# Merging the two root exponentials of a unit, replacing the roots' check by minima, and splitting one copy, in an attention and MLP kernel

## The chip, the cores and the metric

One core of one Trainium2 chip. The metric is the device time of one execution in microseconds (us), median of several runs. A profiled execution of the same program gives the trace; its span is some 1.8 us shorter than the time (605.9 against 607.63 us before). Engines are called PE (TensorE), PEld (its weight loads), ACT (ScalarE), DVE (VectorE), POOL (GpSimd) and SP.

## The reference

Attention with normalised queries and keys (8 batches, 12 heads, 448 positions, 64 columns), then a residual MLP with a layer norm:

```python
def rmsnorm(x, g):
    return x / np.sqrt(np.mean(x * x, axis=-1, keepdims=True) + 1e-06) * g
q_n, k_n = rmsnorm(q, g_q), rmsnorm(k, g_k)
scores = (1.0 / np.sqrt(64)) * np.matmul(q_n, k_n.transpose(0, 1, 3, 2))
attn = softmax(scores)                        # cut: written out with its maximum
x = np.matmul(attn, v) ...                    # to (8, 448, 768)
xn = (x - mu) / np.sqrt(var + 1e-06) * g_ln
out = x + np.maximum(xn @ w_ch1, 0.0) @ w_ch2 # 768 -> 3072 -> 768
```

## The kernel before

Heads are handled in 48 pairs, and the pairs in 25 units (units 0 and 1 hold one pair, the others two). A unit's preparation squares and sums queries and keys, takes the inverse roots, splits the scaled keys in a high and a low half (`khl`) and scales the queries (`qn`). Units 0 to 5 are prepared by a hand-written order at the start, while there is little MLP work to fill PE. The keys' root isn't multiplied into the keys: it is the per-row scale of the score exponential.

```python
def root(n=slice(0, 2)):                      # of unit u; n: queries, keys or both
    nc.scalar.activation(c["rt"][:, n], c["ssq"][:, n], AFT.Ln, bias=D * 1e-6)
    for i in range(2)[n] if isinstance(n, slice) else (n,):
        nc.scalar.activation(c["r", i], c["rt"][:, i], AFT.Exp, scale=-0.5)
# c["r", 0]: a rotating tile "rq" (2 buffers); c["r", 1]: 14 columns of self.rr,
# which keeps the keys' roots of all units (336 columns)

def trans_q(self, p):                         # seven transposes on PE, then one copy
    ...
    if p in ACT_Q:                            # ACT_Q = (0, 1)
        nc.scalar.copy(out=qT, in_=ps.rearrange("p e s -> p (e s)"))

def scores(self, p, i):
    ...                                       # i = 0, 1, 2 use head 0, then 3, 4, 5 head 1, 6 both
    nc.scalar.activation(out=c["E"][:, i], in_=ps[:, 0:S], func=AFT.Exp,
                         scale=self.rr[:, g:g + 1], bias=EXP_BIAS)

def flag(self):                               # near the end: was every root in range?
    ...
    nc.vector.tensor_scalar(out=good[:, 0:nk], in0=self.rr, scalar1=sh.gmax,
                            scalar2=None, op0=ALU.is_ge)
```

The end of the hand-written order, where `M` computes `gmax` on DVE, `m5` duplicates queries, `V6.6` ends pair 6's values, and `K7` transposes and copies pair 7's keys:

```
... N2 R Q7 X2 c5 e5 j5 g5 k5 l5 z5 U1 U2 V6.5 M m5 V6.6 L7 K7
```

Of the kernel before, what the change touches and what calls it, by code (L numbers as in the profile page):

```python
# [8 lines left out]
FP32 = mybir.dt.float32  # L9
FP16 = mybir.dt.float16  # L10
INT32 = mybir.dt.int32
ALU = mybir.AluOpType
AFT = mybir.ActivationFunctionType
AX = mybir.AxisListType
# [7 lines left out]
NPAIR = H // 2  # L22
# [53 lines left out]
class _Fast:  # L76


    def __init__(self, ctx, tc, sh, q, k, v, gs, g_ln, w1, w2, out):
        self.gs, self.g_ln = gs, g_ln  # L80
        self.tc, self.nc, self.sh = tc, tc.nc, sh
        self.q, self.k, self.v, self.w1, self.w2, self.out = q, k, v, w1, w2, out
        nc = tc.nc
        pool = lambda name, bufs, **kw: ctx.enter_context(tc.tile_pool(name=name, bufs=bufs, **kw))
        self.p_in = pool("p_in", 2)
        self.p_n = pool("p_n", 2)
        self.p_e = pool("p_e", 2)
        self.p_x = pool("p_x", 2)
        self.p_xl = pool("p_xl", 2)
        self.p_m = pool("p_m", 1)  # L90
        self.fix = pool("fix", 1)
        self.ps_tr = pool("ps_tr", 1, space=PSUM)
        self.ps_s = pool("ps_s", 2, space=PSUM)
        self.ps_o = pool("ps_o", 1, space=PSUM)
        self.ps_m = pool("ps_m", 3, space=PSUM)
        fix = self.fix
        self.kU = [fix.tile([128, 1920], FP16, name=f"kU{i}", tag=f"kU{i}") for i in range(2)]
        self.qU = [fix.tile([128, 2, 2, S], FP16, name=f"qU{i}", tag=f"qU{i}") for i in range(2)]
        self.v16 = fix.tile([128, 6, 2, 3, D + 1], FP16, name="v16", tag="v16")
        self.vl = fix.tile([128, 6, 2, D + 1], FP16, name="vl", tag="vl")  # L100
        nc.vector.memset(self.v16[:, :, :, :, D], 1.0)
        nc.vector.memset(self.vl, 0.0)
        nc.vector.memset(self.vl[0:64, :, 0, D], 1.0)
        nc.vector.memset(self.vl[64:128, :, 1, D], 1.0)
        self.rec = fix.tile([128, B * NPAIR, 4, 2], FP32, name="rec_all", tag="rec_all")
        nc.vector.memset(self.rec, 0.01)
        self.rr = fix.tile([128, 7 * B * NPAIR], FP32, name="rr_all", tag="rr_all")
        self.rs = fix.tile([128, B, 4], FP32, name="rs_all", tag="rs_all")
        nc.vector.memset(self.rs, RS_LO)
        self.hT = fix.tile([128, NFF, 512], FP16, name="hT", tag="hT")  # L110
        self.tr = self.ps_tr.tile([128, 1024], FP16, name="tr", tag="tr")
        nc.vector.memset(self.tr[:, 64:128].bitcast(FP32), 0.0)
        self.zero_left(DMA_UNIT)
        self.xs, self.xls, self.st = {}, {}, {}
        self.units, self.loads, self.prs = {}, {}, {}
        self.late, self.preps = [], {}
# [71 lines left out]
    def pieces(self, u):  # L188
# [9 lines left out]
        def begin():  # L198
            c["t"] = self.loads.pop(u)
            c["ssq"] = self.p_n.tile([128, 2, 14], FP32, tag="ssq", name="ssq")[:, :, 0:g]  # L200
            c["rt"] = self.p_n.tile([128, 2, 14], FP32, tag="rt", name="rt")[:, :, 0:g]
            o = 7 * UNIT_PAIR[u]
            c["r", 0] = self.p_n.tile([128, 14], FP32, tag="rq", name="rq")[:, 0:g]
            c["r", 1] = self.rr[:, o:o + g]
            c["qn"] = self.p_n.tile([128, 14, 2, D], FP16, tag="qn", name="qn")[:, 0:g]
            c["khl"] = self.p_n.tile([128, 14, 2, D], FP16, tag="khl", name="khl")[:, 0:g]
            self.units[u] = (c["qn"], c["khl"], m)

        def square(n):

# [8 lines left out]

        def root(n=slice(0, 2)):  # L220
            nc.scalar.activation(c["rt"][:, n], c["ssq"][:, n], AFT.Ln, bias=D * 1e-6)
            for i in range(2)[n] if isinstance(n, slice) else (n,):
                nc.scalar.activation(c["r", i], c["rt"][:, i], AFT.Exp, scale=-0.5)  # L223

        def kg():
            if u == 0:
# [81 lines left out]
    def trans_k(self, p):  # L308
        nc, sh = self.nc, self.sh
        u, w = PAIR_UNIT[p]  # L310
        qn, khl, m = self.units[u]
        kT, ps = self.kU[PE_SET][:, 960 * (p % 2):960 * (p % 2) + 960], self.tr
        nc.tensor.matmul(ps[:, 0:256].rearrange("p (e o) -> p e o", e=2)[:, :, 0:D],
                         khl[:, self.group(p, 6)], sh.id16, is_transpose=True, start=True, stop=False)
        for i in range(6):
            nc.tensor.matmul(ps[:, 192 + 128 * i:320 + 128 * i], khl[:, self.group(p, i)], sh.id16,  # L316
                             is_transpose=True, start=False, stop=(i == 5))
        nc.vector.tensor_copy(out=kT, in_=ps[:, 0:960])

    def trans_q(self, p):  # L320
        nc, sh = self.nc, self.sh
        u, w = PAIR_UNIT[p]
        qn, khl, m = self.units[u]
        tr = self.ps_m.tile([128, 1024], FP16, tag="mlp", name="psQ") if p < NPAIR else self.tr
        ps = tr[:, 128:128 + 2 * S].rearrange("p (e s) -> p e s", e=2)
        qT = self.qU[PE_SET][:, p % 2].rearrange("p e s -> p (e s)")
        nc.tensor.matmul(ps[:, :, 384:S], qn[:, self.group(p, 6)], sh.id16, is_transpose=True,
                         start=True, stop=False)
        for i in range(6):
            nc.tensor.matmul(ps[:, i // 3, ts(i % 3, 128)], qn[:, self.group(p, i)], sh.id16,  # L330
                             is_transpose=True, start=False, stop=(i == 5))
        if p in ACT_Q:
            nc.scalar.copy(out=qT, in_=ps.rearrange("p e s -> p (e s)"))
        else:
            nc.vector.tensor_copy(out=qT, in_=ps.rearrange("p e s -> p (e s)"))
        kT = self.kU[PE_SET][:, 960 * (p % 2):960 * (p % 2) + 960]
        self.prs[p] = dict(q=qT, main=kT[:, 192:960], left=kT[:, 0:192])

    def scores(self, p, i):

        nc = self.nc
        c = self.prs[p]
        q, left = c["q"], c["left"]
        if i == 0:
            c["E"] = self.p_e.tile([128, 7, S], FP16, tag="E", name="E")
        if p > UNIT_PAIR[DMA_UNIT] and (7 * p + i) % 3 == 2:
            ps = self.ps_tr.tile([128, 512], FP32, tag="tr", name="psS3")
        else:
            ps = self.ps_s.tile([128, 512], FP32, tag="psS", name="psS")
        if i < 6:  # L350
            h = i // 3
            nc.tensor.matmul(ps[:, 0:S], c["main"][:, ts(i, 128)], q[:, ts(h, S)],  # L352
                             start=True, stop=True)
        else:
            nc.tensor.matmul(ps[:, 0:S], left[:, 0:128], q[:, 0:S], start=True, stop=False)  # L355
            nc.tensor.matmul(ps[:, 0:S], left[:, 64:192], q[:, S:2 * S], start=False, stop=True)  # L356
        g = 7 * UNIT_PAIR[PAIR_UNIT[p][0]] + self.group(p, i)
        nc.scalar.activation(out=c["E"][:, i], in_=ps[:, 0:S], func=AFT.Exp,  # L358
                             scale=self.rr[:, g:g + 1], bias=EXP_BIAS)

    def values(self, p, i):
        nc = self.nc
# [50 lines left out]
    def first_attention(self):  # L413
# [7 lines left out]
        for x in ORDER:  # L421
# [12 lines left out]
            elif key in "SV":  # L434
                (self.scores if key == "S" else self.values)(*map(int, n.split(".")))
            elif key in "KQT":
                dict(K=self.trans_k, Q=self.trans_q, T=self.stats)[key](int(n))
            elif key in "ANXR":
                ln = ln or self.ln_ops(0)
                ln[x]()  # L440
            elif key == "M":
                gmax = self.sh.gmax
                nc.vector.tensor_reduce(out=gmax, in_=self.sh.gprod, axis=AX.X, op=ALU.max,
                                        apply_absolute_value=True)
                nc.vector.tensor_scalar(out=gmax, in0=gmax, scalar1=1.0 / K_MAX, scalar2=None,
                                        op0=ALU.mult)
            elif key == "U":
                self.up_first(int(n))
            elif key == "H":
                ps = self.ps_m.tile([128, 512], FP32, tag="mlp", name="psW")  # L450
                for _ in range(int(n)):
                    nc.tensor.matmul(ps[:, 0:384], self.sh.id16,
                                     self.v16.rearrange("p s h j d -> p (s h j d)")[:, 0:384],
                                     start=True, stop=True)
            else:
                self.prep_ops(int(x[-1]))[x[:-1]]()
# [480 lines left out]
```

## Time and profile before

| | before |
|---|---|
| time, median of the first three runs | 607.91 us (607.86 to 608.15) |
| span of the profiled run | 605.9 us |
| PE busy / PE's first key transpose / PE without waits from | 578.3 us / 8.49 us / 66.04 us |

The page gives busy time and share of the span by engine; the slices divide the span in 40, and a 9 is 90% or more. A line of the timeline is: start, duration, engine, source line, operation, output, input, and in brackets the idle time just before it and what ended that. Two rows of PE, from the timeline of PE between 60 and 67 us:

```profile
60.93 0.55 PE L352 MATMUL psS<-qU,kU 128*128 128x448 f16 x2 [0.46 <-DVE kU L318]
66.04 0.35 PE L352 MATMUL psS<-qU,kU 128*128 128x448 f16 x1 [0.17 <-ACT E L358]
```

The first are the first scores of pair 7, which waited for DVE's copy of the keys. The second are the sixth scores of pair 7, which waited for an exponential of ACT. After this row PE never waits again: I call it PE's steady point.

### The profile page before, as it was taken

The numbers are of one execution on the slowest core, as the hardware profiler recorded it, in microseconds if no ns is written. First come the engines' busy times: TensorE is split into PE (matmuls) and PEld (weight loads), VectorE is DVE, ScalarE is ACT, GpSimd is POOL, SyncE is SP. The second block draws the span as 40 slices with busy tenths as digits, with TensorE's granted clock in tenths as the row PEclk, the third lists the DMA queues.
The fourth block names the chain that finished last, engine by engine and source line by source line (L and its number), as shares of the span: only waits on it lengthen the run. The fifth ranks groups of instructions, "written<-read, shape, count | busy, mean of one in ns | idle before, by whom it ended". The sixth has DMA issues, their size and how long they took to land.

```text
span 605.9 us, 11525 instructions
## 1 busy us (share of the span) xinstructions
PE 578.3 (95%) x4500; PEld 344.6 (57%) x4500; DVE 286.5 (47%) x618; ACT 360.7 (60%) x697; POOL 189.5 (31%) x245
## 2 busy tenths in 40 slices
PE   2877999999999999999999999999999999999995
PEld 1555666655566666655566666655566666654564
DVE  5799567734346256715256255734256322540011
ACT  6996986278752697358753598548754477124200
POOL 3853432233551355332542345423512000000000
PEclk9999999999999999999999999999999999999998
DMA  9999999479864586844944585847722330130011
GB/s 208 266 213 217 215 224 178 123 195 87 143 157 117 98 129 146 177 135 83 150 121 113 123 125 128 197 116 121 133 65 70 92 62 2 34 98 0 1 53 57
DMA packets 130861, 75.29 MB, mean 124 GB/s; under 512 B 96656, under 2 KB 121040, under 8 KB 130800
## 3 DMA queue, kind: packets, MB, share of 16 engines
q1 hardware_dynamic: 114048, 45.12, 38.3%
q0 software_dynamic: 16080, 28.94, 21.6%
q8 instruction: 37, 0.61, 0.4%
q10 hardware_dynamic: 672, 0.43, 0.2%
q14 instruction: 24, 0.20, 0.1%
HBM read 52.36 MB, written 11.01 MB: 105 GB/s over the span
## 4 chain that ended last, share of the span: by engine, by line
PE 88%; DVE 1%; ACT 1%; issue 0%
PE psC L637 36%; PE psH L621 34%; PE psS L352 8%; PE oA L381 5%; PE oB L383 2%; PE psS L356 1%; PE psS L355 1%; PE tr L330 0%; PE tr L316 0%; ACT E L358 0%; DVE x L398 0%; DVE qn L67 0%; DVE khl L240 0%; ACT khl L215 0%; ACT hT L623 0%
## 5 line engine op out<-in xcount | busy, mean ns | idle before, releaser
L621 PE MATMUL psH<-xnT,w 128*128 128x512 f16 (+1 forms) x1134 | 241.9, 353 | 0.0
L358 ACT ACTIVATE E<-psS,rr_all 128x448 f16<-128x448 f32 x336 | 207.0, 634 | 48.3 <-PE psS L352 43.0
L637 PE MATMUL psC<-w,hT 128*128 128x384 f16 (+1 forms) x1368 | 234.7, 323 | 0.0
L623 ACT ACTIVATE hT<-psH 128x512 f16<-128x512 f32 (+1 forms) x189 | 104.0, 550 | 123.9 <-PE psH L621 121.9
L637 PEld LDWEIGHTS <-hT 128*128 128x128 f16 x1368 | 127.5, 98 | 74.6
L621 PEld LDWEIGHTS <-w 128*128 128x128 f16 x1134 | 102.5, 98 | 80.9 <-issue 0.3
L352 PE MATMUL psS<-qU,kU 128*128 128x448 f16 x288 | 100.6, 357 | 8.3 <-ACT E L358 6.0
L381 PEld LDWEIGHTS <-E 128*128 128x128 f16 x1008 | 70.7, 98 | 49.1 <-issue 4.4
L229 POOL TENSOR_TENSOR qkv<-qkv,gprod 128x896 f32<-128x896 f32 x21 | 43.7, 2081 | 95.8 <-issue 49.5
L381 PE MATMUL oA<-v,E 128*128 128x65 f16 x864 | 66.7, 194 | 0.1
L641 DVE SCALAR_TENSOR_TENSOR x<-psC,rs_all,x 128x384 f32<-128x384 f32 x48 | 29.0, 616 | 71.5 <-PE psC L637 71.1
L396 DVE RECIPROCAL rec_all<-oA 128x6 f32<-128x6 f32 x48 | 9.3, 194 | 94.4 <-PE oA L381 94.2
L383 PE MATMUL oB<-v,E 128*128 128x65 f16 x288 | 51.9, 194 | 0.1
L127 POOL DMA_DIRECT2D qkv<-in_k_dram x14 | 11.2, 798 | 129.7 <-DVE qn L279 61.8
L218 DVE TENSOR_REDUCE ssq<-khl 128x14 f32<-128x896 f32 (+1 forms) x24 | 25.6, 1065 | 44.6 <-ACT khl L215 44.5
L352 PEld LDWEIGHTS <-kU 128*128 128x128 f16 x288 | 28.0, 98 | 25.5 <-issue 6.0
L218 DVE TENSOR_REDUCE ssq<-qn 128x14 f32<-128x896 f32 (+1 forms) x25 | 26.2, 1047 | 21.8 <-ACT qn L215 21.7
L67 DVE SCALAR_TENSOR_TENSOR qn<-qkv,rq 128x256 f16<-128x256 f32 (+1 forms) x72 | 26.3, 425 | 15.1 <-ACT rq L223 15.0
L383 PEld LDWEIGHTS <-E 128*128 128x128 f16 x336 | 32.5, 97 | 0.3 <-DVE xl L403 0.2
L240 DVE TENSOR_TENSOR khl<-qkv,khl 128x896 f16<-128x896 f32 x21 | 22.8, 1088 | 10.8 <-ACT khl L237 7.1
L398 DVE TENSOR_TENSOR x<-oA,rec_all 128x384 f32<-128x384 f32 x48 | 26.8, 558 | 1.5
L545 DVE BATCH_NORM_STATS2 stat<-x 128x6 f32<-128x256 f32 (+1 forms) x75 | 26.2, 404 | 0.6
(104 smaller groups left out, 447.7 us busy)
## 6 DMA issues: line engine op xcount, KB each, us to landing
out_dram<-x SPq DMA_DIRECT2D x20, 384.0 KB, 2.5
qkv<-in_k_dram POOLq DMA_DIRECT2D x14, 384.0 KB, 3.9
qkv<-in_q_dram POOLq DMA_DIRECT2D x14, 384.0 KB, 5.2
qkv<-in_v_dram POOLq DMA_DIRECT2D x14, 384.0 KB, 6.6
w<-in_moe_w_ch_dram POOLq DMA_DIRECT2D x3, 1536.0 KB, 14.6
w<-in_moe_w_ch_dram POOLq DMA_DIRECT2D x2, 2304.0 KB, 24.3
qkv<-in_k_dram SPq DMA_DIRECT2D x7, 384.0 KB, 5.7
qkv<-in_q_dram SPq DMA_DIRECT2D x7, 384.0 KB, 4.6
```

The lines of the kernel that those rows point to most:

```text
L67: nc.vector.scalar_tensor_tensor(out=out, in0=x, scalar=8.0, in1=r.unsqueeze(2).broadcast_to([x.shape[0], g, D]), op0=ALU.mult, op1=ALU.mult)
L218: nc.vector.tensor_reduce(out=c["ssq"][:, n], in_=c["sq", n], axis=AX.X, op=ALU.add)
L229: (nc.vector if u in DVE_KG else nc.gpsimd).tensor_tensor(out=c["t"][1], in0=c["t"][1], in1=sh.gprod.unsqueeze(1).broadcast_to([128, g, D] ...
L352: nc.tensor.matmul(ps[:, 0:S], c["main"][:, ts(i, 128)], q[:, ts(h, S)], start=True, stop=True)
L358: nc.scalar.activation(out=c["E"][:, i], in_=ps[:, 0:S], func=AFT.Exp, scale=self.rr[:, g:g + 1], bias=EXP_BIAS)
L381: nc.tensor.matmul(oA[:, t, cs], E[:, i, ts(t, 128)], rhs, start=(i == 0 and t == 0), stop=(i == 6 and t == 2))
L383: nc.tensor.matmul(oB[:, cs], E[:, i, 320:448], rhs, start=(i == 0), stop=(i == 6))
L398: nc.vector.tensor_tensor(out=x[:, :, 128 * hp:128 * hp + 128].rearrange("p t (e d) -> p t e d", e=2), in0=oA[:, :, :, 0:D], in1=rec[:, 0: ...
L621: nc.tensor.matmul(ps[:, 0:N], sh.w1[:, dc, ts(f, 128)], xnT[:, dc, 0:N], start=(dc == 0), stop=(dc == NDC - 1))
L623: nc.scalar.activation(out=hT[:, f, 0:N], in_=ps[:, 0:N], func=AFT.Relu)
L637: nc.tensor.matmul(ps[:, 0:g[1]], hT[:, f, ts(t, 128)], sh.w2[:, f, cols], start=(f == 0), stop=(f == NFF - 1))
L641: nc.vector.scalar_tensor_tensor(out=x[:, cols], in0=ps[:, 0:g[1]], scalar=self.rs[:, b, t:t + 1], in1=x[:, cols], op0=ALU.mult, op1=ALU.add)
```

## The change

The intent: one Exp on 28 columns for queries and keys of a unit in place of two on 14, which needs both roots in one tile. That tile is small and rotates through six buffers, so the roots no longer persist, and the closing check gets one minimum per unit, in a tile of 25 columns. Beside it, pair 0's transposed queries are copied head by head, so that the first scores can start on head 0.

```diff
-        self.rr = fix.tile([128, 7 * B * NPAIR], FP32, name="rr_all", tag="rr_all")
+        self.rr = fix.tile([128, len(UNITS)], FP32, name="rr_all", tag="rr_all")
@@ begin
-            c["r", 0] = self.p_n.tile([128, 14], FP32, tag="rq", name="rq")[:, 0:g]
-            c["r", 1] = self.rr[:, o:o + g]
+            c["rb"] = self.p_n.tile([128, 2, 14], FP32, tag="rq", name="rr_all", bufs=6)[:, :, 0:g]
+            c["r", 0], c["r", 1] = c["rb"][:, 0], c["rb"][:, 1]
@@ root
-            for i in range(2)[n] if isinstance(n, slice) else (n,):
-                nc.scalar.activation(c["r", i], c["rt"][:, i], AFT.Exp, scale=-0.5)
+            nc.scalar.activation(c["rb"][:, n], c["rt"][:, n], AFT.Exp, scale=-0.5)
@@ trans_q
-        if p in ACT_Q:
+        if p == 0:
+            for e in range(2):
+                nc.scalar.copy(out=qT[:, S * e:S * e + S], in_=ps[:, e])
+        elif p in ACT_Q:
@@ scores
+        if i == 6 and UNIT_PAIR[u] == p and u > 4:
+            self.least(u)
+
+    def least(self, u):
+        self.nc.vector.tensor_reduce(out=self.rr[:, u:u + 1], in_=self.units[u][3], axis=AX.X,
+                                     op=ALU.min)
@@ first_attention, key "M"
+                for u in range(5):
+                    self.least(u)
                 gmax = self.sh.gmax
```

(The exponential's scale now comes from the unit's own tile.)

More of the change, by code (lines that the diff above doesn't have):

```diff
@@ L201, in begin @@
             c["rt"] = self.p_n.tile([128, 2, 14], FP32, tag="rt", name="rt")[:, :, 0:g]
-            o = 7 * UNIT_PAIR[u]
-            c["r", 0] = self.p_n.tile([128, 14], FP32, tag="rq", name="rq")[:, 0:g]
-            c["r", 1] = self.rr[:, o:o + g]
+            c["rb"] = self.p_n.tile([128, 2, 14], FP32, tag="rq", name="rr_all", bufs=6)[:, :, 0:g]
+            c["r", 0], c["r", 1] = c["rb"][:, 0], c["rb"][:, 1]
             c["qn"] = self.p_n.tile([128, 14, 2, D], FP16, tag="qn", name="qn")[:, 0:g]
             c["khl"] = self.p_n.tile([128, 14, 2, D], FP16, tag="khl", name="khl")[:, 0:g]
-            self.units[u] = (c["qn"], c["khl"], m)
+            self.units[u] = (c["qn"], c["khl"], m, c["r", 1])
         def square(n):
@@ L310, in trans_k @@
         u, w = PAIR_UNIT[p]
-        qn, khl, m = self.units[u]
+        qn, khl = self.units[u][0:2]
         kT, ps = self.kU[PE_SET][:, 960 * (p % 2):960 * (p % 2) + 960], self.tr
@@ L322, in trans_q @@
         u, w = PAIR_UNIT[p]
-        qn, khl, m = self.units[u]
+        qn, khl = self.units[u][0:2]
         tr = self.ps_m.tile([128, 1024], FP16, tag="mlp", name="psQ") if p < NPAIR else self.tr
@@ L356, in scores @@
             nc.tensor.matmul(ps[:, 0:S], left[:, 64:192], q[:, S:2 * S], start=False, stop=True)
-        g = 7 * UNIT_PAIR[PAIR_UNIT[p][0]] + self.group(p, i)
+        g = self.group(p, i)
         nc.scalar.activation(out=c["E"][:, i], in_=ps[:, 0:S], func=AFT.Exp,
-                             scale=self.rr[:, g:g + 1], bias=EXP_BIAS)
+                             scale=self.units[PAIR_UNIT[p][0]][3][:, g:g + 1], bias=EXP_BIAS)
+        u = PAIR_UNIT[p][0]
+        if i == 6 and UNIT_PAIR[u] == p and u > 4:
[3 more added lines that the diff above has]
+                                     op=ALU.min)
     def values(self, p, i):
```

## The prediction

> **What bounds the kernel now.** I read the page first (busy shares, the 40 slices, the chain's summary), then busy time by stretch, then the timeline of ScalarE (ACT) and TensorE (PE) in the first 24 us, the chain of waits around 56 to 66 us, and last PE's waits after 61 us. From the page:
>
> ```profile
> PE 578.3 (95%) x4500; PEld 344.6 (57%) x4500; DVE 286.5 (47%) x618; ACT 360.7 (60%) x697; POOL 189.5 (31%) x245
> PE   2877999999999999999999999999999999999995
> PE 88%; DVE 1%; ACT 1%; issue 0%
> ```
>
> PE is full from about the fifth slice (15 us each) on; the only stage with holes is the start, where the attention of batch 0 runs with little MLP work to fill PE. Busy time by stretch (us from the start; then PE, PEld, DVE, ACT, POOL) says the same more finely:
>
> ```profile
> 15.00:20.00 5.00, 4.21 (x28) 2.59 (x28) 3.34 (x4) 4.76 (x11) 4.33 (x6) 1.00 1.11 333
> 25.00:30.00 5.00, 3.93 (x43) 2.47 (x43) 4.81 (x10) 4.90 (x13) 3.85 (x6) 1.00 0.85 212
> 50.00:55.00 5.00, 3.22 (x50) 2.74 (x49) 3.89 (x6) 2.81 (x6) 2.65 (x4) 1.00 1.12 221
> 70.00:600.00 530.00, 529.40 (x3980) 312.56 (x3978) 231.03 (x508) 303.56 (x582) 151.89 (x199) 1.00 0.56 112
> ```
>
> From 70 to 600 us PE is busy 529.4 of 530 us: nothing on ACT or VectorE (DVE) can shorten that part, only a new stall can lengthen it. Before that, ACT binds from 12 to about 24 us (4.76 of 5), ACT and DVE both are full from 24 to 40 us (4.90 and 4.81), and from 45 to 61 us DVE leads, with short round trips over PE and ACT. PE's waits after 61 us add up to 0.7 us, in two pieces:
>
> ```profile
> PE psS L352 <- DVE kU L318: 0.5, 1, 0.5
> PE psS L352 <- ACT E L358: 0.2, 1, 0.2
> ```
>
> So the change can pay or cost only in the first 66 us, and each instruction must be judged by whether it lies on ACT before 24 us or on DVE after that.
>
> [...] the Ln on 28 columns takes 240 ns, the Exp on 14 takes 215 and 198 ns. [...] an Exp recorded with 0.22 us is followed by the next after 0.12 us. So I count the step from start to start, not the recorded time. [...] The ACT timeline:
>
> ```profile
> 10.31 0.91 ACT L333 COPY qU<-psQ 128x896 f16<-128x896 f16 x1
> 11.12 0.21 ACT L221 ACTIVATE rt<-ssq 128x7 f32<-128x7 f32 x1
> 11.36 0.21 ACT L223 ACTIVATE rr_all<-rt 128x7 f32<-128x7 f32 x1
> 11.90 1.16 ACT L358 ACTIVATE E<-psS,rr_all 128x448 f16<-128x448 f32 x2 [0.33 <-PE psS L352]
> ...
> 18.65 0.22 ACT L223 ACTIVATE rq<-rt 128x14 f32<-128x14 f32 x1
> 18.77 0.20 ACT L223 ACTIVATE rr_all<-rt 128x14 f32<-128x14 f32 x1
> 18.88 2.21 ACT L358 ACTIVATE E<-psS,rr_all 128x448 f16<-128x448 f32 x4
> ```
>
> and PE's answer to the copy:
>
> ```profile
> 11.27 0.91 PE L352 MATMUL psS<-qU,kU 128*128 128x448 f16 x2 [0.99 <-ACT qU L333]
> ```
>
> **The change part by part.**
>
> (1) The copy of pair 0, 128x896 in one, becomes two of 128x448. ACT copies of PSUM took 482 ns for 384 columns, 798 for 768, 905 for 896: about 0.83 ns a column, so 448 columns are an estimated 0.535 us, start to start about 0.43 (two of 384 columns took 0.86 in all, hence 0.38 apart). The first half ends at 10.31 + 0.535 = 10.85, where the whole ended at 11.22. The first scores need head 0 alone, so they start at about 10.9 instead of 11.27 and finish at about 11.45. But their exponential also waits for its scale, the root of the keys: the second copy runs 10.74 to 11.28, the Ln starts at about 11.18 (11.12 now), its Exp at 11.42, and the first score exponential, which reads that Exp, about 0.24 later (the Ln to Exp distance): 11.66 instead of 11.90. **Gain 0.24 us**; if the first half needn't wait for the transposes of head 1 it starts 0.14 earlier, and the gain is up to 0.37.
>
> (2) Two Exps on 14 columns become one on 28. Start to start: Ln 18.39, Exp 18.65, Exp 18.77, next 18.88. One Exp of 28 columns will record about 0.23 us and hold ACT for some 0.13, so each merged unit gives back 0.12 + 0.11 - 0.13 = **0.10 us of ACT**. Unit 0 calls its roots apart and gains nothing. Of 25 units 24 gain, 2.4 us of ACT in all, but on the path lie only units 1 and 2 (at 12.95 and 18.39, in ACT's full stretch): 0.2 us; units 3 and 4 fall where DVE is as full as ACT (ACT waits for DVE at 40.50), unit 5 in a stretch where ACT had 2.65 us to spare; unit 6, at 65.15, is on the chain just ahead of PE's 0.2 us wait: 0.1 us. **Gain 0.3 us.** The queries' root arrives some 0.01 us later than alone: nothing.
>
> (3) The check of the roots' size takes a minimum per unit instead of all 336 columns. In its place come 24 reductions of 128x14 to 128x1 on DVE. DVE reductions took 155 ns for 3 columns, 186 for 32, 214 for 64: about 0.17 us recorded for 14, and start to start about 0.09 (a recorded 1.08 is followed after 1.00). Nineteen, 3.2 us, lie in the PE-bound part beside a DVE busy 231 of 530 us: hidden. The closing check gets shorter by about 0.5 us (395 + 493 ns for 336 columns, to about 0.36 for 24), at 534 us, while PE runs on: nothing. But **five stand in the schedule at "M"**, ahead of gmax, and there the chain runs on DVE (start, us, what):
>
> ```profile
> 57.34 1.00 DVE qn L67
> 58.34 0.14 DVE gmax L443
> ...
> 60.21 0.67 DVE kU L318
> 60.88 0.04 issue
> 60.93 0.55 PE psS L352 x2
> ```
>
> Pair 7's keys are copied at the end of this run of DVE work, and PE has waited 0.46 us for that copy. Five times 0.09 is **0.45 us lost** (0.85 if they don't overlap, at the recorded 0.17).
>
> Sum: -0.24 - 0.3 + 0.45 = about **-0.1 us**, from 607.91 to some 607.8.
>
> **The rivals.** (a) The ACT gain doesn't arrive. DVE has no hole over 0.15 us between 24 and 40 us; if its start at 23.89 doesn't come earlier, 0.44 us of the gain is lost, and the five minima show in full: 608.3. For it speaks that DVE is so full; against it that DVE's start there waits for PE's V0.6, and PE for ACT's exponentials (0.41 us at 23.34), so the whole row should move. (b) The minima cost little, being independent of their neighbours, and the copy gives its larger value: 607.3. (c) DVE's order after the start isn't by hand, and the 19 new reductions may be placed so that an evacuation comes late and PE stalls. Against it: PE waited for DVE only once after 61 us, so buffers leave slack. It would cost tenths, not microseconds. (d) The new tile with 6 buffers makes a unit's Exp wait for the minimum of the unit six earlier. That minimum is issued many microseconds before; no wait is likely.
>
> **Range and chances.** Best case about -0.37 - 0.3 + 0.3 = -0.4, with timing noise of 0.15 (three runs spread 607.86 to 608.15) perhaps -0.7; worst case (a) with minima at their recorded time +0.8. So 607.7 as the middle, weighting the earlier first copy a little, and 607.0 to 608.5 for 8 in 10. Two per cent are 12 us: the stage that can change is 66 us long and all it loses to waits of PE is some 20 us, so neither side is within reach of half a microsecond of edits. Faster 0.005, same 0.985, slower 0.01.
>
> **What would show it right or wrong.** Two copies of about 0.53 us at 10.2 to 10.8, the first scores near 10.9 and the first score exponential near 11.6 (right for part 1). A root group in 0.39 us from Ln to the next instruction where it took 0.49 (part 2). DVE at 23.9 us starting 0.4 to 0.5 earlier (rival a refuted if so). Five reductions of about 0.17 us before gmax, 0.09 apart, and the copy of pair 7's keys near its old 60.2 (part 3). PE's waits after 66 us still near nothing (rival c). The prediction would be wrong if the minima brought a wait with them, if the clock of PE warmed at another moment of the start (score matmuls take 0.53 us before 19 us and 0.35 after), or if a long DVE reordering opened holes in PE.

The sum is -0.24 us for the copy, -0.3 for the merged Exp and +0.45 for the minima, about -0.1 us, each from steps and waits in the trace of before.

## The result and the profile after

The kernel after took a median of 608.56 us in six runs (607.48 to 608.80), the kernel before 608.07 us in six (607.86 to 609.48, the first three included). The ratio is 0.9999 with a 95% interval of 0.9986 to 1.0012: the same. A ratio is the mean time of one kernel's fast runs over that of the other's in the same rounds, so it isn't quite the ratio of the medians. The median lies 0.06 us above the upper end of the predicted range, but both kernels spread over more than 1 us, which three runs of before had not shown. So a question comes before that of the change: what makes the same program differ by 1 us? The traces answer both.

The page of the kernel after:

```profile
PE 578.2 (95%) x4500; PEld 345.2 (57%) x4500; DVE 287.0 (47%) x643; ACT 359.3 (59%) x674; POOL 190.1 (31%) x245
```

DVE has 25 instructions more (one minimum a unit; the prediction counted 24 and 19 where it is 25 and 20), ACT 23 fewer (24 merged roots, one copy more), and PE the same work. The timeline of ACT after, start and unit 2:

```profile
10.57 0.97 ACT L333 COPY qU<-psQ 128x448 f16<-128x448 f16 x2 [0.93 <-PE psQ L329]
11.43 0.22 ACT L220 ACTIVATE rt<-ssq 128x7 f32<-128x7 f32 x1
11.68 0.21 ACT L221 ACTIVATE rr_all<-rt 128x7 f32<-128x7 f32 x1
11.92 1.16 ACT L360 ACTIVATE E<-psS,rr_all 128x448 f16<-128x448 f32 x2
...
18.32 0.23 ACT L220 ACTIVATE rt<-ssq 128x28 f32<-128x28 f32 x1
18.58 0.23 ACT L221 ACTIVATE rr_all<-rt 128x28 f32<-128x28 f32 x1
18.72 2.21 ACT L360 ACTIVATE E<-psS,rr_all 128x448 f16<-128x448 f32 x4
```

At first sight nothing is gained: the first score exponential starts at 11.92 where it was 11.90. But this execution began later: the first key transpose of PE, which waits for the first inputs, is at 8.75 us against 8.49. Counted from there, the exponential comes after 3.17 us instead of 3.41. Unit 2's root group takes 0.40 us from its Ln to the next instruction where it took 0.49. Then DVE after, at 24 us and at the end of the start:

```profile
23.74 0.20 DVE L407 RECIPROCAL rec_all<-oA 128x6 f32<-128x6 f32 x1
...
58.10 0.44 DVE L369 TENSOR_REDUCE rr_all<-rr_all 128x1 f32<-128x7 f32 x5
58.46 0.21 DVE L456 TENSOR_REDUCE gmax<-gprod 128x1 f32<-128x64 f32 x1
58.59 0.16 DVE L369 TENSOR_REDUCE rr_all<-rr_all 128x1 f32<-128x14 f32 x1
58.70 0.15 DVE L458 TENSOR_SCALAR gmax<-gmax 128x1 f32<-128x1 f32 x1
...
60.41 0.66 DVE L317 COPY kU<-tr 128x960 f16<-128x960 f16 x1
```

The five minima stand where they were expected and hold DVE for 0.36 us (58.10 to 58.46), 0.072 each. A sixth, unit 5's, was placed by the scheduler between the two steps of `gmax`, where DVE stood waiting for its own result anyway (0.25 us from step to step before, 0.24 now). And PE:

```profile
61.13 0.55 PE L354 MATMUL psS<-qU,kU 128*128 128x448 f16 x2 [0.86 <-DVE kU L317]
...
65.87 0.35 PE L354 MATMUL psS<-qU,kU 128*128 128x448 f16 x1
```

PE waits 0.40 us longer for pair 7's keys, and yet it reaches its steady point earlier, 65.87 against 66.04, and doesn't wait there.

To compare traces I take the distances between five points: the first key transpose of PE (F), DVE's first reciprocal, at 24 us (R), DVE's subtraction for unit 5's keys, at 56 us (H), DVE's copy of pair 7's keys, at 60 us (K), PE's sixth scores of pair 7, its steady point (S), and PE's last instruction. All in us:

| trace | F at | F to R | R to H | H to K | H to S | F to S | S to PE's last |
|---|---|---|---|---|---|---|---|
| before | 8.49 | 15.40 | 32.37 | 3.95 | 9.78 | 57.55 | 533.60 |
| after | 8.75 | 14.99 | 32.36 | 4.31 | 9.77 | 57.12 | 533.61 |

From F to S the change saves **0.43 us**; PE's remaining 533.6 us are the same to 0.01. F came 0.26 later (it lies anywhere from 8.36 to 9.00 us in our traces, with the landing of the inputs), which leaves the 0.2 us by which the spans differ (605.9 and 605.7).

### The profile page after: what moved, and what is told of

Same layout as the page of the kernel before. It is cut to its first block, busy times and chain, and to the rows that moved or that the text cites. A ratio compares the mean times of both kernels' runs of the same rounds, so it can differ in the third digit from the quotient of the medians.

```text
span 605.7 us, 11526 instructions
## 1 busy us (share of the span) xinstructions
PE 578.2 (95%) x4500; PEld 345.2 (57%) x4500; DVE 287.0 (47%) x643; ACT 359.3 (59%) x674; POOL 190.1 (31%) x245
## 4 chain that ended last, share of the span: by engine, by line
PE 90%; DVE 2%; ACT 0%; issue 0%; DVEq 0%
PE psC L650 36%; PE psH L634 35%; PE psS L354 8%; PE oA L392 5%; PE oB L394 2%; PE psS L357 1%; PE psS L358 1%; PE tr L329 0%; PE tr L315 0%; PE psU L680 0%; DVE stat L558 0%; DVE xn L579 0%; DVE x L409 0%; DVE qU L337 0%; ACT E L360 0%
## 5 line engine op out<-in xcount | busy, mean ns | idle before, releaser
L67 DVE SCALAR_TENSOR_TENSOR qn<-qkv,rr_all 128x256 f16<-128x256 f32 (+1 forms) x72 | 26.3, 423 | 15.3 <-ACT rr_all L221 15.3
```

Of the source, the lines that this page charges most:

```text
L67: nc.vector.scalar_tensor_tensor(out=out, in0=x, scalar=8.0, in1=r.unsqueeze(2).broadcast_to([x.shape[0], g, D]), op0=ALU.mult, op1=ALU.mult)
```

## Experiments

My theory after this: (1) ACT's time before 24 us passes to the end one for one, through R; (2) from R to H DVE sets the pace, and roots of units 3, 4 and 5 are off the path; (3) the minima delay K by their full time, and part of this meets slack at S, where ACT's chain is about as late; (4) the 1 us between runs has another cause. The rivals: DVE's full row holds the pace whatever ACT did before it (so the 0.41 us at R would be chance), or S is set by ACT alone and K doesn't matter. Twelve kernels ran, each beside the kernel before on the same chip, all correct. The distances of all traces are here, for the sections below:

| trace | F to R | R to H | H to K | H to S | F to S | S to PE's last |
|---|---|---|---|---|---|---|
| a_control (before again) | 16.09 | 32.34 | 3.96 | 9.79 | 58.22 | 533.60 |
| b_split | 15.82 | 32.36 | 3.96 | 9.78 | 57.96 | 533.59 |
| c_merge | 15.22 | 32.36 | 3.96 | 9.65 | 57.23 | 533.60 |
| d_moved | 14.99 | 32.37 | 3.96 | 9.65 | 57.01 | 533.60 |
| e_min8 | 15.88 | 32.36 | 8.68 | 16.80 | 65.04 | 533.61 |
| f_exp_early | 20.61 | 32.44 | 4.32 | 9.78 | 62.83 | 533.61 |
| g_exp_u5 | 14.99 | 32.37 | 6.54 | 13.86 | 61.22 | 533.60 |
| h_min_main | 16.03 | 32.37 | 4.31 | 9.77 | 58.17 | 534.09 |
| i_min3 | 15.00 | 32.36 | 5.03 | 10.48 | 57.84 | 533.60 |
| j_exp12 | 16.92 | 32.37 | 4.31 | 9.77 | 59.06 | 533.59 |
| k_exp345 | 15.02 | 32.36 | 4.31 | 9.84 | 57.22 | 533.60 |
| l_exp6 | 15.03 | 32.38 | 4.31 | 10.23 | 57.64 | 533.60 |

### The control: the kernel before against itself

No edit. Label a_control.

> The kernel before, unchanged, against itself: the noise of a comparison. Ratio 1.000 within 0.001, single times between about 607.4 and 609 us as in the runs so far. In its trace the first score exponential starts at about 11.9 us and the copy of pair 7's keys at 60.2, both moved together by however much later the first input lands (0.26 us between the two traces so far).

Measured: 608.33 us against 608.18, ratio 1.0002 (0.9988 to 1.0016). So a comparison of five rounds can't see less than about 0.8 us. The trace is of more use: the same program took 0.69 us longer from F to R than in the trace of before, so here I was wrong that points move together with the inputs alone. The cause stands in the timeline of PE, score matmuls of before and then of the control:

```profile
19.54 0.35 PE L352 MATMUL psS<-qU,kU 128*128 128x448 f16 x1 [0.43 <-ACT E L358]
22.06 0.35 PE L352 MATMUL psS<-qU,kU 128*128 128x448 f16 x1
```

and the control:

```profile
20.95 0.56 PE L352 MATMUL psS<-qU,kU 128*128 128x448 f16 x1
22.59 0.56 PE L352 MATMUL psS<-qU,kU 128*128 128x448 f16 x1
23.91 0.37 PE L352 MATMUL psS<-qU,kU 128*128 128x448 f16 x1
```

In both, score matmuls take 0.53 to 0.56 us at first and 0.35 later, but the change comes at about 18.7 us in one execution and at about 23.9 in the other. The clock records of the traces say the same: the first one, the turn to full clock, stands at 18.76 us in before and at 23.94 in the control. The two rates are a factor of two apart (the two matmuls of a seventh score start 0.37 us apart at 17.35 us and 0.19 apart at 23.87 in before), and the moment of the turn differs by 5 us between two executions of the same program; what sets it, no run shows. Before, after, c_merge, d_moved, g, i, k and l turned fast early (first record at 18.1 to 19.4 us); the control, b, e and j late (23.6 to 24.4); h and f turned early (17.9 and 20.1) and fell back once before 31 us. Only traces that turned alike may be compared from F to R.

With F anywhere from 8.36 to 9.00 us, 0.7 to 0.9 us for a late turn (0.69 here, 0.65 in b_split, 0.89 in e_min8, each against what its parts give with an early turn), and 6.2 to 6.6 us from PE's last instruction to the end of the span, up to some 1.9 us can come together. The kernel before spread by 1.3 to 1.6 us on each of the three chips of these experiments, so these three could account for all of it. That they do isn't shown: how often each occurs in unprofiled runs stays open, as these leave no trace.

### Only the copy split

```diff
-        if p in ACT_Q:
+        if p == 0:
+            for e in range(2):
+                nc.scalar.copy(out=qT[:, S * e:S * e + S], in_=ps[:, e])
+        elif p in ACT_Q:
```

> Only pair 0's copy in two halves, all else as before. Theory (ACT time before 24 us reaches the end): counted from the first key transpose, the first score exponential comes 0.24 us earlier (3.17 instead of 3.41 us), VectorE's row at 23.9 us and the copy of pair 7's keys come 0.24 earlier too, and the time falls by about 0.2 us. Rival (VectorE's full row holds the pace): the first exponential earlier by 0.24, but the row at 23.9 us and the key copy unmoved, no time gained.

Measured: 607.95 against 608.18 us, ratio 0.9995 (0.9982 to 1.0009), which decides nothing. Its trace turned late, like the control's: the first score exponential is at 3.17 us from F instead of 3.41, F to R 0.27 us shorter (15.82 against 16.09), F to S 0.26 shorter. The two clocks didn't turn at quite the same place (15.35 us after F in the control, 15.06 here, where the work is 0.24 us ahead too), so a pair that turned early is the better witness: up to R, c_merge and the change differ by the copy alone, and F to R is 15.22 and 14.99, 0.23 apart. The theory holds: the 0.24 us won at 12 us are still there at 24 us, and in b_split at 66 us.

### Only the merged exponential

The change with the copy undone and `least` empty; the tile that the check reads is filled with a constant, so this kernel checks less.

```diff
+        nc.vector.memset(self.rr, 1.0)
@@ least
-        self.nc.vector.tensor_reduce(...)
+        pass
```

> Only the merged exponential; the copy undone, and no minima at all (the check of the roots is fed with a constant, so this kernel checks less but gives the same output). Theory: counted from the first key transpose, VectorE's row at 23.9 us 0.2 us earlier, the copy of pair 7's keys 0.2 earlier, TensorE steady 0.2 to 0.3 us earlier, time about 0.3 us less. Rival: key copy unmoved, time unchanged.

Measured: 607.83 against 608.18 us, ratio 1.0 (0.9986 to 1.0013). The trace turned early, like that of before: F to R 0.18 us shorter, R to H unchanged, H to S 0.13 shorter, F to S **0.32 us** shorter in all. The two parts of the gain lie where the prediction had put them: units 1 and 2, and unit 6. (Unit 5's root, at 56.4 us, lies in H to S as well; k_exp345 below shows that it counts for little.) That R to H is the same to 0.01 shows that the merged roots of units 3 and 4, which lie in it, gain nothing.

### The minima moved

The key `Y` stands where DVE waits 0.59 us for PE:

```diff
-... R Q7 X2 c5 e5 j5 ...
+... R Q7 Y X2 c5 e5 j5 ...
@@ first_attention
-            elif key == "M":
+            elif key == "Y":
                 for u in range(5):
                     self.least(u)
+            elif key == "M":
```

> The whole change with the five minima moved from ahead of gmax to VectorE's wait ahead of the copy of batch 0's third transposed tile (0.59 us idle there). Theory: the five minima cost 0.36 us of VectorE's row at 58 us and fit into the wait, so the copy of pair 7's keys comes 0.36 us earlier than in the change as it is, counted from the first key transpose; of this 0.1 to 0.36 reaches the point where TensorE runs without waits (66 us) and the end. Rival: ScalarE's row sets that point anyway, the key copy moves and TensorE's steady point does not.

Measured: 608.02 against 608.18 us, ratio 1.0 (0.9986 to 1.0014). In the trace the five minima fill the wait (0.23 us of it is left), H to K is back at 3.96, 0.35 less than in the change, and H to S is 9.65, which is 0.12 less. So of 0.36 us only **0.12 us** reach the steady point. The minima and the key copy in DVE's timeline, then the first scores of pair 7 in PE's:

```profile
53.59 0.44 DVE L369 TENSOR_REDUCE rr_all<-rr_all 128x1 f32<-128x7 f32 x5
...
59.69 0.66 DVE L317 COPY kU<-tr 128x960 f16<-128x960 f16 x1
...
60.40 0.55 PE L354 MATMUL psS<-qU,kU 128*128 128x448 f16 x2 [0.50 <-DVE kU L317]
```

From these scores to S PE takes 4.98 us here and in c_merge (60.40 to 65.38 here), and 4.74 in the change (61.13 to 65.87): the difference, 0.24 us, is time that PE lost there and that the later keys used up. This kernel has the shortest start of all, F to S 57.01, 0.54 less than before. By the clock it can't be told from the others; by the traces it is the best version that keeps the check.

### Forty minima

```diff
-                for u in range(5):
-                    self.least(u)
+                for u in range(40):
+                    self.least(u % 5)
```

> The change with its five minima ahead of gmax issued eight times over, 35 reductions more. Theory (VectorE's row at 58 us leads to the copy of pair 7's keys, and TensorE waits for that copy): at 0.073 us each, as the six steps from 58.10 to 58.46 and on show, some 2.5 us more in VectorE's row, the copy 2.5 us later, the steady point of TensorE later by nearly all of it, at least 2.2 us, and the time up by as much, to about 610.5. Rival (the row has slack, ScalarE sets the steady point): the copy 2.5 us later, the steady point by less than 1 us.

Measured: 614.36 against 608.64 us, ratio 1.0091 (1.0075 to 1.0108), twice what I expected. It isn't a clean dose. H to K grew by 4.37 us: 2.49 for the 35 minima, about 1.0 because the scheduler now put unit 6's sum of squares ahead of the query duplication, and 1.0 because that duplication took 1.40 us instead of 0.38 (why, no run shows). PE then waited 5.23 us and came back slow, as its timeline shows:

```profile
66.46 0.93 PE L354 MATMUL psS<-qU,kU 128*128 128x448 f16 x2 [5.23 <-DVE kU L317]
67.17 2.13 PE L634 MATMUL psH<-xnT,w 128*128 128x384 f16 x6
```

Six MLP matmuls take 2.13 us there and 1.14 in the change, and the granted clock from 66 to 70 us is 0.50. It came back slow after a wait of 5.23 us, and in g_exp_u5 below at nearly the same place after one of 2.37 us; how long a wait it takes, no run shows. Direction right, size useless; the dose was repeated smaller below (i_min3).

### More exponentials early

```diff
-            nc.scalar.activation(c["rb"][:, n], c["rt"][:, n], AFT.Exp, scale=-0.5)
+            for _ in range(11 if u in (1, 2) else 1):
+                nc.scalar.activation(c["rb"][:, n], c["rt"][:, n], AFT.Exp, scale=-0.5)
```

> The change with ten repeats of the merged exponential in units 1 and 2, 20 more on ScalarE before 19 us, at about 0.12 us each (unit 1 has 14 columns, unit 2 has 28): 2.4 us. Theory (ScalarE's full row before 24 us sets VectorE's row after it, and so the end): VectorE's row at 23.7 us, the copy of pair 7's keys and the steady point all 2.2 to 2.6 us later, time about 610.5. Rival (VectorE holds the pace from 24 us on whatever ScalarE did before): the row moves by under 1 us, time about 608.5.

Measured: 612.98 against 608.64 us, ratio 1.0071 (1.0055 to 1.0088). My dose was wrong: eleven such Exps, each writing the tile of the one before, took 2.69 and 2.80 us, 0.26 each and not 0.12. Twenty more are 5.1 us, and F to S is 5.71 longer, with PE fallen back to its slow clock at 23.5 us, in a wait of 3.01 us, until 30.4. The theory's side, but two things are mixed.

### More exponentials in unit 5

As above with `u == 5`.

> The change with ten repeats of the merged exponential in unit 5, at 56.5 us, 1.3 us more on ScalarE at a place where it had 2.65 us of idle time just before but a chain of work behind it. Theory of the prediction (unit 5's exponential is off the path): the copy of pair 7's keys comes at the same distance from the first key transpose, within 0.1 us, and time is unchanged. Rival (ScalarE's work from 56 to 66 us sets the steady point of TensorE): the copy unmoved, but the steady point later by 0.5 to 1.3 us.

Measured: 611.82 against 608.64 us, ratio 1.0053 (1.0036 to 1.0069). A miss. The same mistake made the dose 2.57 us, and this exceeds what is free: DVE's query scaling waited 2.13 us for the root, K came 2.22 later, and ACT's Relus behind it held up PE by 2.37. And PE came back slow: its clock was 0.50 from 60.28 to 63.69 us. First the change, then this run:

```profile
57.18 3.09 PE L634 MATMUL psH<-xnT,w 128*128 128x384 f16 x18
...
59.97 4.76 PE L635 MATMUL psH<-xnT,w 128*128 128x384 f16 x18 [2.37 <-ACT hT L685]
```

The same eighteen matmuls take 1.67 us longer, so the 4.09 us more from H to S are a wait and a slow clock together, and not a measure of the root's cost. Unit 5's root is off the path by a few tenths, not by the 2.65 us of idle time that I read just before it: idle time ahead of an instruction says when it could start, not how late it may end.

### Ten times the minima in the main part

```diff
-            self.least(u)
+            for _ in range(10):
+                self.least(u)
```

> The change with each of the 20 minima after the start issued ten times, 180 reductions or some 16 us more on VectorE in the stretch where TensorE is full. Theory (hidden): from the steady point to TensorE's last instruction it is 533.6 us as in all six traces so far, within 0.1, and the time is unchanged at 607.3 to 608.9. Rival (they delay evacuations): that stretch longer by 0.5 us or more, with waits of TensorE for VectorE in it.

Measured: 608.48 against 608.64 us, ratio 0.9995 (0.9979 to 1.0012). From S to PE's last it is 534.09 us, 0.49 more than in every other trace; my theory had allowed 0.1. One place makes it up, as a comparison of PE's starts with those of the change shows; here the waits between 100 and 110 us:

```profile
PEld L393 <- DVE x L410: 0.5, 1, 0.5
```

(Columns: who waited for whom, us in total, times, longest.) A row of seven minima stood ahead of DVE's evacuation of a pair's attention output, and PE's weight load waited for that evacuation once. These repeats started 0.20 us apart and not 0.072, so DVE's busy time grew by 27.6 us (314.6 against 287.0) where 16 were expected. In the runs with forty and fifteen minima neighbours write different columns; here each writes the column of the one before, which is the likely reason. So 180 minima cost 0.5 us, and the 20 of the change cost nothing that shows (533.61 against 533.60). Hidden, but not for any number of them.

### Fifteen minima

As e_min8 with `range(15)` and `u % 5`; here DVE's order is otherwise that of the change.

> The five minima ahead of gmax three times over, 10 reductions more at the 0.073 us that the run with forty showed for one; VectorE's order is otherwise that of the change, which it wasn't in that run. Theory: from pair-8 keys' subtraction (khl, about 56 us) to the copy of pair 7's keys 0.73 us more than the change's 4.31, that is 5.04, TensorE's wait for the copy 1.6 instead of 0.9, its steady point later by 0.73 counted from the same subtraction (9.77 in the change, 10.50 here). Rival: ScalarE sets the steady point and takes up part, under 0.4 later.

Measured: 609.30 against 608.69 us, ratio 1.0013 (0.9996 to 1.0029). In the trace H to K 5.03 (5.04 expected), H to S 10.48, which is 0.71 more than in the change. The minima in DVE's timeline and the first scores of pair 7 in PE's:

```profile
58.13 1.15 DVE L369 TENSOR_REDUCE rr_all<-rr_all 128x1 f32<-128x7 f32 x15
...
61.87 0.55 PE L354 MATMUL psS<-qU,kU 128*128 128x448 f16 x2 [1.57 <-DVE kU L317]
```

Each minimum beyond the five of the change costs its whole 0.072 us at the steady point. The first five cost 0.12 of 0.36: the slack at S is 0.24 us, and the change had used it up. From pair 7's first scores to S PE takes 4.74 us here as in the change, without a wait: that is its own work, and nothing is left to take up.

### Independent exponentials early

```diff
+            for i in range(8 if u in (1, 2) else 0):
+                nc.scalar.activation(self.dummy[:, i, :, 0:g], c["rt"][:, 0:2], AFT.Exp, scale=-0.5)
```

> Eight extra exponentials in each of units 1 and 2, into a spare tile's separate columns, so that none waits for the one before (in the earlier run with repeats into one tile each took 0.26 us and not 0.12): 16 times 0.12 to 0.13, 2.0 us on ScalarE before 24 us. Theory: third square group of ScalarE, VectorE's row at 24 us and the steady point all about 2.0 us later than in a run of the change whose TensorE turns fast at the same place (steady point 57.1 us after the first key transpose if it turns before 20 us, about 57.7 after 23 us): 59.1 to 59.8. Time up by about 2 us. Rival (VectorE's row has its own pace): under 1 us.

Measured: 609.51 against 608.69 us, ratio 1.0014 (0.9997 to 1.0031). ACT took 0.93 and 1.02 us for the two groups of eight. In the trace F to R 16.92 and F to S 59.06, that is 1.93 and 1.94 us more than in the change. Not all of it is the dose, as PE turned fast late in this trace (24.43 us). The last group of eight and the score exponentials behind it:

```profile
19.65 1.02 ACT L224 ACTIVATE dummy<-rt 128x28 f16<-128x28 f32 x8
20.57 2.39 ACT L363 ACTIVATE E<-psS,rr_all 128x448 f16<-128x448 f32 x4
```

From start to start the groups hold ACT for 0.83 and 0.92 us, 1.75 together (0.11 an Exp). The four score exponentials take 2.39 us, as in the control, which turned late too, and 2.21 in the change: the other 0.18. From ACT's next square to R it is 2.91 us as in the change and in before. So ACT's time, dose and late clock together, reaches R one for one, and DVE's row follows. The rival (under 1 us) is out.

### Independent exponentials in units 3, 4 and 5

As above, two in each of units 3, 4 and 5.

> Two extra independent exponentials, 0.25 us, in each of units 3, 4 and 5. Theory (these units' roots are off the path): from VectorE's row at 24 us to khl at 56 us 32.36 us as in the change and in before (32.36 to 32.37 in four of the traces), and from khl to the steady point 9.77 as in the change; nothing gained or lost, each within 0.1. Rival (ScalarE is as full as VectorE there and both hold the path): up to 0.5 us more in the first stretch, 0.25 in the second.

Measured: 607.86 against 608.69 us, ratio 0.9992 (0.9975 to 1.0009). R to H 32.36, unchanged by 0.5 us more on ACT; H to S 9.84, 0.07 more than the change for 0.25 us in unit 5. The roots of units 3 and 4 are off the path, unit 5's all but.

### Independent exponentials in unit 6

As above, four in unit 6.

> Four extra independent exponentials, 0.5 us, in unit 6 at 65 us, just ahead of a score exponential that TensorE's next scores wait for. Theory (ScalarE's chain sets the steady point to within 0.1 to 0.2 us there): from khl to the steady point 9.77 plus 0.3 to 0.5, and TensorE shows a wait of that size for the score exponential at the steady point. Rival (unit 6 is off the path in the change, as TensorE shows no wait there): within 0.1 of 9.77.

Measured: 608.05 against 608.69 us, ratio 0.9990 (0.9973 to 1.0007). H to S is 10.23, 0.46 more than in the change for four Exps of about 0.12, and PE's wait is back at the steady point. First the four Exps in ACT's timeline:

```profile
65.26 0.56 ACT L224 ACTIVATE dummy<-rt 128x28 f16<-128x28 f32 x4
```

then the sixth scores of pair 7 in PE's, which wait for the score exponential behind them:

```profile
66.39 0.35 PE L357 MATMUL psS<-qU,kU 128*128 128x448 f16 x1 [0.38 <-ACT E L363]
```

So in the change both chains, ACT's and DVE's with PE behind it, reach S at nearly the same moment, and either can lengthen it.

## Why the prediction was right or wrong

**The bound and the scale: right.** From the steady point to PE's last instruction it is 533.59 to 533.61 us in thirteen of the fourteen traces; only ten times the minima moved it. "Same" follows, and the ratio is 0.9999.

**The copy: right in mechanism and size.** 0.24 us predicted, 0.24 at the first score exponential and 0.26 at the steady point in the run that had it alone, and 0.23 at R between two traces that turned early. The larger value (0.37, if the first half need not wait for head 1) did not come: the copy waited 0.93 us for PE's transposes and started after the last of them.

**The merged exponential: right.** 0.3 us predicted, in units 1, 2 and 6 alone; 0.18 and 0.13, sum 0.32 as measured, and nothing from units 3 and 4. Two readings beside it were off and did no harm: unit 5's root has a few tenths of a microsecond to spare and not 2.65 (g_exp_u5, k_exp345), and the minima are 25, of which 20 come after the start, not 24 and 19.

**The minima: the term that was mis-sized.** The prediction said "Five times 0.09 is 0.45 us lost". DVE's row grew by 0.36 us, 0.072 each, and of this only 0.12 us reached PE's steady point. The step that failed is the passage from DVE's row to the end: the 0.46 us wait of PE for the key copy was read as the end of the only chain, though the prediction itself had noted PE's 0.2 us wait for ACT five microseconds later, and used it for unit 6. ACT's chain was the later of the two at S, by 0.24 us once the roots were merged, and a delay of DVE is first taken from that slack. The sum was therefore -0.1 us in place of the traces' -0.43 (-0.41 before R, nothing from R to H, -0.13 for unit 6, +0.12 for the minima).

**Rival (a) is refuted** (DVE's row at 24 us moves by all of ACT's gain, and j_exp12 shows it with a dose of 1.75 us). Rival (b) was half right: the minima cost little, but the copy gave its smaller value. Rivals (c) and (d) left no sign in the change.

**The range was too narrow for its reason.** It took the noise from three runs that spread by 0.3 us. The runs of the kernel before spread by up to 1.6 us on one chip, and one likely cause was named at the end of the prediction as something that would make it wrong (PE's clock turning at another moment): in the traces of the control, b_split, e_min8 and h_min_main F to R was 0.65 to 1.04 us longer, more than the change moves anything. That the median came out within 0.06 us of the range is partly luck: the 0.43 us that the traces show for the change is below what these runs can resolve.

## What to carry to other kernels

Before asking what an instruction costs, ask at which point of the program the engines next all wait for one of them, and how late each chain arrives there: a delay on the chain that isn't last costs only what exceeds the slack, and here 0.36 us on DVE cost 0.12. When an effect is smaller than the spread of the times, compare distances between fixed points of traces, take a control trace of the unchanged kernel, and compare only traces in which PE's clock turned at the same place. In a dose experiment, make the extra instructions independent and small enough that neither the scheduler's order nor the clock changes.

## What the traces show of the engines beside this

- Independent small Exps on ACT are recorded with 0.20 to 0.23 us and start 0.12 us apart (18.65 and 18.77 us in before; eight in 1.02 us in j_exp12). A row of them into the same tile goes slower: 0.26 us each, eleven in 2.69 and 2.80 us (f_exp_early).
- The same on DVE: minima into the same column started 0.20 us apart (h_min_main), where those into different columns were 0.072 apart (fifteen in 1.15 us, i_min3).
- PE's clock turned at 18.76 us in one execution and at 23.94 in another of the same program, and the start was 0.7 us longer; and in four traces PE fell back to slow once after it had turned fast. It fell back in waits of 5.23 us (e_min8) and 3.01 us (f_exp_early), after one of 2.37 us (g_exp_u5), and in h_min_main at 21.28 us with no wait of PE longer than 0.8 us near it (score matmuls 0.35 us at 20.56, 0.56 at 22.63). What did it in h_min_main stays open.
- A trace may hold no clock record before the first turn: the first one stands at 18.76 us in before, and the views print a granted clock of 1.00 ahead of it, with score matmuls of 0.53 us; after a fall back they print 0.50 (66 to 70 us in e_min8).
